# Out-projection results kept in the other half of u, PSUM banks rotated by two between stages, and another set of planner keys

## Chip, cores and metric

The kernel runs on one core of a Trainium2 chip. The metric is the device time of one execution in microseconds. Before the change it is 513.69 us (median of three runs, 512.78 to 514.52).

## What is computed

For a batch of 8, causal attention over 576 positions with 8 heads of width 64: heads 0 to 3 look at the last 32 positions (local), heads 4 to 7 at every 32nd position (strided). The eight heads side by side are x, and a gated MLP with a spatial mixing follows:

```python
scores = q @ k.T / 8, masked per head; attn = softmax(scores); x = heads of attn @ v side by side   # 576 x 512
h = relu(x @ w_in);  u, v = h[:, :512], h[:, 512:]
v_n = (v - mean(v)) / sqrt(var(v) + 1e-6)
v_s = w_spatial @ v_n + b_spatial[:, None]
out = (u * v_s) @ w_out
```

w_in, w_spatial and w_out arrive in wider types; every fp32 product is made of three fp32r matmuls (high by high, high by low, low by high), so each operand exists as a rounded half and a rest.

## The kernel before

**Stages.** Each batch b has four attention tiles (two heads each, two local and two strided) and then, on TensorE, the stages v (`project_v`, 48 matmuls of 512 columns), u (`project_u` for batches 0 and 1, `project_u_blocks` for 2 to 7), tail (`moe_tail`), s (`gate`, the spatial product times u) and o (`project_out`). From batch 2 on the order is v(b), o(b-1), u(b), the tail for every second b, s(b). Attention of the next batch or two is laid between them.

**u and o by seven products.** `project_u_blocks` and `project_out` compute a 2 by 2 block product with seven products "11", "s1", "s2", "s4", "s3", "12", "22" instead of eight. Each product is 12 matmuls of 288 columns into a pair of PSUM banks. "11", "s2", "s3" and "22" go into the pair xb, "s1" and "s4" into zb, "12" into wb. After "11" the pair xb is copied out (`keep`), and "s2" then adds on top of it in the same banks; in the same way zb is copied out after "s1" before "s4" adds to it. In u the copies after "11" are written to the first half of u, u[0] blocks 0 and 1, and those after "s1" to u[1] blocks 2 and 3. "11", "s4" and "12" of u read x directly, the others need a sum that is cast and subtracted first (`split`: a cast on ScalarE or GpSimd, L409 or L411, and a subtraction on VectorE, L419).

**Buffers.** u(b) is a pair of tiles from the ring `r_u`, which has two buffers, so u[0] of batch b has the buffer that u[0] of batch b-1 had, and u[1] that of u[1]; batch 1 has its u in two x buffers. The first access to a new tile waits for every operation on the old tile of that buffer, whichever blocks they touch (`Buf.before`). o(b-1) puts its last two results ("22", copied out of xb) into u[1] blocks 0 and 1 and stores them from there to `out` in HBM, 144 KB each.

**Banks.** The ring `r_pm` has four PSUM banks, taken in turn. In u and o, xb takes two, zb the next two; xb is held, so wb takes zb's two again. After "22" the hold is cleared, and the next stage begins with xb's banks.

**The order of everything** is made by a planner (`Program.order`) ahead of the run: each operation has a key, and each engine in turn takes the ready operation with the smallest key, where readiness is the planner's own estimate (a DMA counts as done 1600 ns and 900 ns and its transfer time after its issue). `KEYS` holds these numbers: "a" is the key of attention tiles 0 to 7 (batches 0 and 1), "la" and "lb" that of their q, k and v loads, "lv", "lu", "lo", "ls" that of the weight loads, "v", "u", "wv", "wu", "s", "t", "o" that of the conversion of the weights, "su" that of `in_weight_sums` (the sums of w_in blocks that u's products need from batch 2 on). "lead" is how long ahead of its use an attention tile from batch 2 on is due, "pre"[0] how far a `split` is put ahead of its product, "pre"[1] the same for the differences, "dp" by how much a choice of VectorE is penalised for each kind of operation. The stages of batches 0 to 7 have keys from 0 to 375; o(0) begins at 63.6, s(1) at 73.9, v(2) at 87.7 and u(2) at 108.4. Each engine and the one DMA queue (SP) then runs its list strictly in order.

Of the kernel before, what the change touches and what calls it, by code (L numbers as in the profile page):

```python
# [37 lines left out]
TAIL = S - 4 * P  # L38
NT = 4
KEYS = {  # L40
    "a": (-3398.1, -3117.71, -3291.55, -2240.6, -1996.2, 35.64, -1043.59, -1504.49,),
    "v": (691.31, 1274.34, 186.27, 627.47,),
    "u": (1079.81, 934.5, -4091.05, -677.5,),
    "s": (-2936.24, 1502.92, 3125.66, -518.81,),
    "t": (-1209.93,),
    "o": (2379.44, 1239.03,),
    "cst": (-2116.05,),
    "wv": (-860.51, -882.07, -3005.6, 768.52,),
    "wu": (1507.37, -2412.73, 850.89, 747.53,),
    "lead": (10.96,),  # L50
    "fill": (-727.48, 2496.32, -2940.02, 1257.47, 970.88, -749.94,),
    "dp": (601.61, -9631.11, 16122.32, 30415.43,),
    "dpt": (806.42,),
    "lv": (-1842.4, -1199.82, -515.75, 336.68,),
    "lu": (3197.26, 951.54, 884.39, 816.26,),
    "lo": (-770.37, -754.89, 1060.46, -3432.48,),
    "ls": (-921.47, 216.61, -1263.15, 1069.04, 606.92,),
    "pre": (1.57, 46.46,),
    "su": (-798.11,),
    "near": (3759.3,),  # L60
    "la": (-1978.67, -1285.55, -2262.03, -1136.47, -309.0, 2452.66, 231.16, 2175.93,),
    "lb": (-364.89, 1312.27, -646.09, 1254.93, 2634.11, -1849.12, -3019.6, -2748.21,),
}
WARM_END, WARM_GAP, WARM_COST, WARM_COLS, WARM_SHARE = 110000.0, 700.0, 427.0, 256, 0.8
PE_MASKED, APART = (0, 1, 2, 3), ()
# [92 lines left out]
class Program:  # L158
# [10 lines left out]
    def add(self, key, choices, fn, reads=(), writes=(), spare=None, tiled=0, port=(), kind=0):  # L169


        n = len(self.ops)
        if port:
            self.port[n] = port
        self.kind[n] = kind
        if spare is not None:
            self.spare[n] = spare
        if tiled:
            self.tiled[n] = tiled
        deps = set()  # L180
        for tok in reads:
            if tok in self.writer:
                deps.add(self.writer[tok])
            self.readers.setdefault(tok, []).append(n)
        for tok in writes:
            if tok in self.writer:
                deps.add(self.writer[tok])
            deps.update(self.readers.pop(tok, ()))
            self.writer[tok] = n
        for tok in (*reads, *writes):  # L190
            buf = tok[0]
            if isinstance(buf, Buf):
                deps.update(buf.before)
                buf.users.append(n)
        deps.discard(n)
        self.ops.append((key, choices, fn, deps))
# [143 lines left out]
def pe_cost(m, n):  # L340
    return max(m / 1.2, 4.8 + 0.4464 * n)
# [3 lines left out]
def attention_moe(ctx, tc, qT, kT, ks, vl, vs, cst, eye, w_in, w_out, wsp, wtail, out):  # L345
# [49 lines left out]
    r_pm = Ring(ps, "m", [P, 512], F32, 4)  # L395
    held, lead = set(), min(nb, 2)
# [29 lines left out]
    def evac(key, n, dst, src, reads, writes, engs=(ACT, DVE), extra=0):  # L426
        cost = {ACT: 60 + 0.833 * n + extra, DVE: 70 + 1.04 * n + extra}

        def fn(eng):
            if hasattr(eng, "activation"):  # L430
                eng.copy(dst(), src())  # L431
            else:
                eng.tensor_copy(dst(), src())

        add(key, [(e, cost[e]) for e in engs], fn, reads, writes)
# [376 lines left out]
    def x_tok(t):  # L812
        return [(xs[t], i, c0) for i in range(1 if t in WHOLE else 2) for c0 in ((0, 3) if t % NHP < 2 else (0, 1))]
# [55 lines left out]
    def split(key, n, dst, tok, val, toks):  # L869
        rnd(key, n, lambda: dst(0), val, toks, [(*tok, 0)])  # L870
        rest(key, n, lambda: dst(1), val, lambda: dst(0), toks + [(*tok, 0)], [(*tok, 1)])
# [277 lines left out]
    def project_u_blocks(b, key):  # L1149
        at, tok = sums.pop(b)  # L1150
        u = [r_u.new() for _ in range(2)]
        us[b, 0], us[b, 1] = u
        step = 1.5

        def product(key, name, src, bank, first):
            w_at, w_tok = in_sums[name]
            for r in range(2):
                op, toks = src(r, key + 0.74 * r)
                for j in range(2):

                    def fn(eng, r=r, j=j, op=op):
                        for i, (w, a) in enumerate(PROD):
                            eng.matmul(  # L1163
                                bank[j]()[:, :HS], w_at(w, r)[:, j * P : (j + 1) * P], op(a),
                                start=(first and r == 0 and i == 0), stop=(r == 1 and i == 2),
                                skip_group_check=not first,
                            )

                    add(
                        key + 0.74 * r + 0.37 * j, [(PE, 3 * pe_cost(P, HS))], fn,  # L1170
                        toks + w_tok[r], [(bank[j],)],
                    )

        def direct(k, hf):
            return lambda r, key: (
                lambda a: xs[NHP * b + 2 * k + r]()[:, a, hf * HS : hf * HS + HS], x_tok(NHP * b + 2 * k + r),
            )

        def summed(n, slot):
            def src(r, key):  # L1180
                g = gs[slot]
                op = lambda a: g()[:, 2 * r + a]
                split(key - KEYS["pre"][0], HS, op, (g, r), at(n, r), tok(n, r))
                return op, [(g, r, 0), (g, r, 1)]
            return src

        def keep(key, hf, f, bank):
            evac(key, HS, block(u[hf], f), lambda: bank()[:, :HS], [(bank,)], [(u[hf], f)])

        def join(key, hf, f, bank):  # L1190
            dst = block(u[hf], f)
            add(
                key, [(DVE, 70 + 1.04 * HS)],
                lambda eng: eng.tensor_tensor(dst(), bank()[:, :HS], dst(), op=ALU.add),  # L1194
                [(bank,)], [(u[hf], f)],
            )

        xb, zb = ([r_pm.new(held) for _ in range(2)] for _ in range(2))
        held.update(x.n % 4 for x in xb)
        product(key, "11", direct(0, 0), xb, True)  # L1200
        product(key + step, "s1", summed(0, 1), zb, True)
        for j in range(2):
            keep(key + step, 0, j, xb[j])
        product(key + 2 * step, "s2", summed(1, 0), xb, False)
        for j in range(2):
            keep(key + 2 * step, 1, 2 + j, zb[j])
        product(key + 3 * step, "s4", direct(1, 1), zb, False)
        for j in range(2):
            keep(key + 3 * step, 1, j, xb[j])
        product(key + 4 * step, "s3", summed(2, 1), xb, False)  # L1210
        for j in range(2):
            join(key + 4 * step, 1, j, zb[j])
        wb = [r_pm.new(held) for _ in range(2)]
        product(key + 5 * step, "12", direct(1, 0), wb, True)
        for j in range(2):
            join(key + 5 * step, 1, 2 + j, xb[j])
        product(key + 6 * step, "22", summed(3, 0), xb, False)
        held.clear()
        for j in range(2):
            join(key + 6 * step, 0, j, wb[j])  # L1220
            keep(key + 7 * step, 0, 2 + j, xb[j])
# [44 lines left out]
    def block(u, f):  # L1266
        return lambda: flat(u)[:, f * HS : (f + 1) * HS]
# [50 lines left out]
    def project_out(b, key):  # L1318
        u = [us.pop((b, hf)) for hf in range(2)]
# [34 lines left out]
        def keep(key, dst, bank, writes):  # L1354
            evac(key, HS, dst, lambda: bank()[:, :HS], [(bank,)], writes)
# [8 lines left out]
        def store(key, e, hf, src, reads):  # L1364
            c0 = b * S + hf * HS
            add(
                key, [(DMA, P * HS * 4 / DMA_RATE)],
                lambda eng: eng.dma_start(out[e * P : (e + 1) * P, c0 : c0 + HS], src()),
                reads, [],
            )  # L1370
# [7 lines left out]
        mine = lambda hf, f: block(u[hf], f)  # L1378
        step = 1.47
# [28 lines left out]
        xb, zb = ([r_pm.new(held) for _ in range(2)] for _ in range(2))  # L1408
# [29 lines left out]
            store(key + 5 * step, 2 + j, 1, o5[j], [(o5[j],)])  # L1438
        multiply(key + 6 * step, "22", [(0, 0), (0, 1)], xb, 0, False)
        held.clear()  # L1440
        for j in range(2):
            join(key + 6 * step, o1[j], wb[j], [(o1[j],)])
            store(key + 6 * step, j, 0, o1[j], [(o1[j],)])
        for j in range(2):
            keep(key + 7 * step, mine(1, j), xb[j], [(u[1], j)])
            store(key + 7 * step, 2 + j, 0, mine(1, j), [(u[1], j)])

    gs = []
    plan = []
# [199 lines left out]
```

## Time and profile before

| | us |
|---|---|
| median of three runs | 513.69 |
| the profiled execution | 517.83 |
| its span, first to last instruction | 515.8 |
| TensorE busy in the span | 492.4 (95%) |
| VectorE busy | 409.2 (79%) |
| ScalarE busy | 288.2 (56%) |
| GpSimd busy | 132.7 (26%) |

Times below are microseconds from the start of the span. PE is TensorE's matmul stream, PEld its weight load, DVE VectorE, ACT ScalarE, POOL GpSimd, SPq the DMA issue queue. In a timeline the figure in brackets is the idle time of the engine just before, and what ended it. Several equal instructions in a row are merged into one line, with their count.

### The profile page before, as it was taken

Reading aid. Unit: us, or ns where it says so; the run is one execution under the profiler, and the core shown is the slowest. Engines: PE = TensorE matmul, PEld = TensorE weight load, DVE = VectorE, ACT = ScalarE, POOL = GpSimd, SP = SyncE. Lnnn points to the kernel's source line nnn. Section 1 sums busy time; section 2 is a strip of 40 time slices with the busy share of each in tenths; the row PEclk is TensorE's granted clock in tenths of the full one; section 3 lists DMA queues with packets and bytes.
Section 4 is the critical chain, followed back from the end, with each engine's and each line's share of the span. In section 5 each row is a group of like instructions: output and inputs, shape, how many; then the busy total and the mean of one; then the engine's idle time right before and its main releaser. Section 6 shows DMA issues by size and latency. Waiting matters only on the chain.

```text
span 515.8 us, 16002 instructions
## 1 busy us (share of the span) xinstructions
PE 492.4 (95%) x6330; PEld 447.1 (87%) x6330; DVE 409.2 (79%) x1268; ACT 288.2 (56%) x899; POOL 132.7 (26%) x269
## 2 busy tenths in 40 slices
PE   6698999999999999999999989999899999999997
PEld 3466898898988989998998978989899998889997
DVE  4899989999999878887797947979588775658455
ACT  5797778556466738266553737527464562227314
POOL 4563343323033223121231112311122201111000
PEclk9699999999999999999999989999999999999999
DMA  8995232223421444004430244202441032001102
GB/s 292 398 376 157 74 131 81 78 89 108 155 79 48 141 132 141 17 11 139 157 122 2 71 153 128 79 0 65 143 120 32 0 97 81 1 0 61 34 0 93
DMA packets 26250, 52.71 MB, mean 102 GB/s; under 512 B 3136, under 2 KB 11584, under 8 KB 26176
## 3 DMA queue, kind: packets, MB, share of 16 engines
q1 hardware_dynamic: 26176, 51.70, 30.6%
q8 instruction: 50, 0.82, 0.7%
q14 instruction: 24, 0.20, 0.1%
HBM read 42.25 MB, written 9.44 MB: 100 GB/s over the span
## 4 chain that ended last, share of the span: by engine, by line
PE 74%; DVE 9%; DMA 7%; ACT 6%; issue 2%; SPq 1%; POOL 0%; ACTq 0%; DVEq 0%
PE m L1284 19%; PE m L1070 17%; PE m L1337 13%; PE m L1163 8%; PE m L1127 5%; PE po L616 3%; PE po L721 3%; DMA outT<-u 2%; PE s L504 2%; ACT pl L561 2%; PE m L1296 2%; PE m L1297 2%; PE s L650 2%; DVE g L419 1%; DMA vn<-w_in 1%
## 5 line engine op out<-in xcount | busy, mean ns | idle before, releaser
L1284 PE MATMUL m<-wsp_sb,vn 128*128 128x288 f32 x768 | 114.4, 297 | 1.6 <-DVE u L1194 1.5
L1284 PEld LDWEIGHTS m<-wsp_sb,vn 128*128 128x128 f32 x768 | 105.6, 188 | 4.1 <-DVE u L1194 2.4
L1070 PE MATMUL m<-w_in_sb,x 128*128 128x512 f32 (+1 forms) x408 | 99.5, 397 | 0.8 <-DVE pp L681 0.4
L1337 PE MATMUL m<-g,w_out 128*128 128x288 f32 x672 | 92.7, 296 | 1.0 <-DVE u L1360 1.0
L1337 PEld LDWEIGHTS m<-g,w_out 128*128 128x128 f32 x672 | 90.3, 188 | 2.5 <-ACT x L431 1.0
L1070 PEld LDWEIGHTS m<-w_in_sb,x 128*128 128x128 f32 (+1 forms) x408 | 74.3, 185 | 19.9 <-DVE x L419 1.0
L409 ACT CAST g<-u 128x288 fp32r<-128x288 f32 x79 | 33.9, 433 | 38.4 <-DVE u L876 20.7
L411 POOL TENSOR_SCALAR ptl<-pc 32x64 f32<-32x64 f32 (+3 forms) x92 | 36.1, 392 | 55.6 <-DVE pc L585 30.2
L1038 POOL TENSOR_TENSOR bn<-bn,cst_sb 128x1 f32<-128x1 f32 (+1 forms) x37 | 22.1, 601 | 108.4 <-DVE bn L1033 96.2
L1020 ACT ACTIVATE vv<-m 128x512 f32<-128x512 f32 (+1 forms) x37 | 21.7, 596 | 49.8 <-PE m L1070 48.7
L561 ACT ACTIVATE pl<-pl,ml 128x64 f32<-128x64 f32 (+1 forms) x140 | 47.1, 340 | 1.5 <-DVE ml L541 1.2
L419 DVE TENSOR_TENSOR g<-u,g 128x288 fp32r<-128x288 f32 x98 | 43.1, 458 | 5.7 <-ACT g L409 5.0
L431 ACT CAST x<-po 128x288 fp32r<-128x288 f32 x62 | 23.4, 402 | 36.0 <-PE po L721 28.2
L409 ACT COPY ptl<-pc 32x320 f32<-32x320 f32 (+3 forms) x100 | 35.9, 359 | 10.6 <-DVE pc L585 8.7
L1163 PE MATMUL m<-x,w_in_sb 128*128 128x288 f32 x216 | 34.6, 301 | 4.4 <-ACT u L431 4.4
L431 ACT COPY u<-m 128x288 f32<-128x288 f32 x76 | 28.1, 402 | 17.4 <-PE m L1163 7.9
L1163 PEld LDWEIGHTS m<-x,w_in_sb 128*128 128x128 f32 x216 | 29.9, 188 | 5.9 <-ACT u L431 5.1
L1025 DVE BATCH_NORM_STATS2 bn<-vv 128x6 f32<-128x512 f32 (+1 forms) x37 | 25.1, 685 | 10.5 <-ACT vv L1020 10.5
L411 POOL TENSOR_SCALAR pts<-pc 32x288 f32<-32x288 f32 x36 | 17.8, 494 | 56.5 <-PE po L721 40.5
L1045 DVE TENSOR_SCALAR vv<-vv,bn 128x512 f32<-128x512 f32 (+1 forms) x37 | 20.6, 557 | 11.8 <-POOL bn L1038 11.3
L419 DVE TENSOR_TENSOR x<-po,x 128x288 fp32r<-128x288 f32 x64 | 27.2, 447 | 2.9 <-ACT x L431 1.6
L1307 DVE SCALAR_TENSOR_TENSOR u<-u,m 128x288 f32<-128x288 f32 x48 | 21.0, 448 | 10.1 <-PE m L1297 10.1
(167 smaller groups left out, 890.6 us busy)
## 6 DMA issues: line engine op xcount, KB each, us to landing
q<-qT SPq DMA_DIRECT2D x32, 295.0 KB, 3.9
v_raw<-vs SPq DMA_DIRECT2D x15, 512.0 KB, 3.6
v_raw<-vl SPq DMA_DIRECT2D x16, 384.0 KB, 3.2
k<-kT SPq DMA_DIRECT2D x16, 304.0 KB, 4.6
kbd<-ks SPq DMA_DIRECT2D x32, 144.0 KB, 4.5
outT<-o SPq DMA_DIRECT2D x32, 144.0 KB, 3.3
outT<-u SPq DMA_DIRECT2D x28, 144.0 KB, 1.9
vn<-w_in SPq DMA_DIRECT2D x4, 512.0 KB, 6.8
```

What stands on the lines that cost most here:

```text
L409: eng.copy(dst(), src())
L411: eng.tensor_scalar(dst(), src(), 1.0, 0.0, op0=ALU.mult, op1=ALU.add)
L419: eng.tensor_tensor(dst(), src(), f32(hi()), op=ALU.subtract)
L431: eng.copy(dst(), src())
L561: eng.activation(p_sb()[:m, u, :], src, AF.Exp, bias=st()[:m, u : u + 1], scale=SCALE if masked else -1.0, **total,)
L1025: lambda eng: eng.bn_stats(bn()[:m, 0:6], v()[:m]), [(v,)], [(bn,)],
L1038: lambda eng: eng.tensor_tensor(bn()[:m, 9:10], bn()[:m, 8:9], sel[:m, 0:1], op=ALU.pow),
L1070: eng.matmul(v_ps()[:m, :], x_at(kt)[:, a, :], w_in_sb[:, w, kt, HF:], start=(n == 0 and i == 0), stop=(n == NT - 1 and i == 2),)
L1127: eng.matmul(u_ps()[:, :HS], w_in_sb[:, w, kt, f * P : (f + 1) * P], xs[NHP * b + kt]()[:, a, r], start=(n == 0 and i == 0), stop=(n == NT ...
L1163: eng.matmul(bank[j]()[:, :HS], w_at(w, r)[:, j * P : (j + 1) * P], op(a), start=(first and r == 0 and i == 0), stop=(r == 1 and i == 2), ...
L1284: eng.matmul(s_ps()[:, :HS], vn()[:, a, kt, fs], wsp_sb[:, w, kt, r], start=(kt == 0 and i == 0), stop=False,)
L1337: eng.matmul(o_ps()[:, :HS], w_out_t[0]()[:, w, r, BLOCKS[name], j * P : (j + 1) * P], at(a), start=(first and r == 0 and i == 0), stop=(r ...
```

## The change

It has three parts: in `project_out` the results of "22" go to u[0] blocks 2 and 3 and are stored from there; after the hold is cleared, in `project_u_blocks` and in `project_out`, the bank counter moves on by two, so that the next stage begins with wb's banks; and all of `KEYS` is replaced, the keys of batches 0 and 1 by those of a kernel with U as eight products.

```diff
 KEYS = {
-    "a": (-3398.1, -3117.71, -3291.55, -2240.6, -1996.2, 35.64, -1043.59, -1504.49,),
-    "v": (691.31, 1274.34, 186.27, 627.47,),
-    "u": (1079.81, 934.5, -4091.05, -677.5,),
+    "a": (-1421.69, -1241.69, -1361.69, -558.71, -62.58, 1238.23, -54.07, 892.52,),
+    "v": (-847.67, 1532.36, -699.97, -197.47,),
+    "u": (1324.65, 1473.2, 1712.36, -439.99,),
...
-    "lead": (10.96,),
+    "lead": (10.06,),
...
-    "dp": (601.61, -9631.11, 16122.32, 30415.43,),
-    "dpt": (806.42,),
-    "lv": (-1842.4, -1199.82, -515.75, 336.68,),
-    "lu": (3197.26, 951.54, 884.39, 816.26,),
+    "dp": (1410.82, -7913.25, 17481.82, 35293.8,),
+    "dpt": (1128.82,),
+    "lv": (-1086.66, -783.28, -283.36, -137.47,),
+    "lu": (1077.79, 1592.36, 778.71, 457.25,),
...
-    "pre": (1.57, 46.46,),
-    "su": (-798.11,),
-    "near": (3759.3,),
-    "la": (-1978.67, -1285.55, -2262.03, -1136.47, -309.0, 2452.66, 231.16, 2175.93,),
-    "lb": (-364.89, 1312.27, -646.09, 1254.93, 2634.11, -1849.12, -3019.6, -2748.21,),
+    "pre": (0, 63.25,),
+    "near": (4678.86,),
+    "la": (-1146.66, -1026.66, -1601.69, -759.97, -1481.69, -1206.66, 298.54, 1013.03,),
+    "lb": (-639.38, 1353.2, -257.47, 1652.36, 1178.23, 517.25, -343.36, 1784.57,),
+    "su": (72.55,),
 }
...
         product(key + 6 * step, "22", summed(3, 0), xb, False)
         held.clear()
+        r_pm.n += 2
...
         multiply(key + 6 * step, "22", [(0, 0), (0, 1)], xb, 0, False)
         held.clear()
+        r_pm.n += 2
...
         for j in range(2):
-            keep(key + 7 * step, mine(1, j), xb[j], [(u[1], j)])
-            store(key + 7 * step, 2 + j, 0, mine(1, j), [(u[1], j)])
+            keep(key + 7 * step, mine(0, 2 + j), xb[j], [(u[0], 2 + j)])
+            store(key + 7 * step, 2 + j, 0, mine(0, 2 + j), [(u[0], 2 + j)])
```

## Rows read from the trace of the kernel before

**Rows 1.** The page's first lines: the span, and TensorE's busy time.

```profile
span 515.8 us, 16002 instructions
...
PE 492.4 (95%) x6330; PEld 447.1 (87%) x6330; DVE 409.2 (79%) x1268; ACT 288.2 (56%) x899; POOL 132.7 (26%) x269
```

**Rows 2.** Busy time of each engine in six stretches of the span: the stretch, its length, then PE, PEld, DVE, ACT and POOL busy with their instructions, TensorE's granted clock as a share, the share of the 16 DMA engines, GB/s.

```profile
0.00:16.60 16.60, 8.79 (x164) 5.09 (x165) 9.22 (x24) 9.11 (x31) 5.82 (x12) 0.86 0.89 317
16.60:25.20 8.60, 8.17 (x232) 5.93 (x232) 7.27 (x17) 7.18 (x28) 6.22 (x11) 0.67 1.04 395
25.20:46.30 21.10, 19.27 (x342) 13.05 (x343) 19.76 (x55) 18.59 (x58) 11.34 (x16) 1.00 0.87 310
46.30:149.00 102.70, 101.74 (x1501) 93.94 (x1500) 96.82 (x335) 68.89 (x229) 34.33 (x66) 1.00 0.32 103
149.00:512.40 363.40, 354.48 (x4099) 329.06 (x4097) 276.09 (x842) 183.98 (x554) 75.03 (x166) 1.00 0.24 73
512.40:515.80 3.40, 0.00 (x0) 0.00 (x0) 0.00 (x0) 0.41 (x2) 0.00 (x0) 1.00 0.34 115
```

**Rows 3.** What TensorE's matmul stream waited for over the whole span: waiting line and releaser, us in total, times, longest us.

```profile
PE m L504 <- DMA vn<-w_in: 6.0, 1, 6.0
PE m L1163 <- ACT u L431: 4.4, 3, 2.2
PE m L1284 <- DVE u L1194: 1.5, 4, 0.4
...
PE m L1337 <- DVE u L1360: 1.0, 1, 1.0
```

**Rows 4.** All engines in order of time from the end of o(3) into u(4); of these lines those of PE, ACT's copies out of PSUM and SPq's stores. PE's lines at 294.43, 295.21 and 297.60 are the first half of "s1", "11" and, after the other half of "s1", "s2"; 301.57 is the beginning of "s4".

```profile
294.43 0.94 PE L1163 MATMUL m<-g,v_raw 128*128 128x288 f32 x6
...
295.21 1.76 PE L1163 MATMUL m<-x,w_in_sb 128*128 128x288 f32 x12
...
296.48 0.98 SPq L1368 DMA_DIRECT2D outT<-u  x2
...
296.93 0.67 ACT L431 COPY u<-m 128x288 f32<-128x288 f32 x2
...
297.60 1.77 PE L1163 MATMUL m<-g,su_sb 128*128 128x288 f32 x12
...
301.12 0.70 ACT L431 COPY u<-m 128x288 f32<-128x288 f32 x2 [2.85 <-DMA outT<-u]
...
301.57 0.66 PE L1163 MATMUL m<-x,w_in_sb 128*128 128x288 f32 x3 [2.20 <-ACT u L431]
```

**Rows 5.** TensorE alone in order of time: a place in o(0); the beginning of "s4" in u(3); the attention product behind the wait of rows 4; the beginning of "s4" in u(5), and the same attention product there; the beginning of u(6) and of its "s4", and the same of u(7).

```profile
127.88 3.40 PE L1337 MATMUL m<-g,w_out 128*128 128x288 f32 x24 [0.96 <-DVE u L1360]
...
241.47 0.66 PE L1163 MATMUL m<-x,w_in_sb 128*128 128x288 f32 x3 [0.80 <-ACT u L431]
...
302.18 2.19 PE L616 MATMUL po<-ptl,v_raw 128*64 128x96 f32 x24
...
365.75 0.66 PE L1163 MATMUL m<-x,w_in_sb 128*128 128x288 f32 x3 [1.37 <-ACT u L431]
366.36 1.21 PE L616 MATMUL po<-ptl,v_raw 128*64 128x96 f32 x24
...
417.73 0.56 PE L1163 MATMUL m<-g,v_raw 128*128 128x288 f32 x3
...
422.50 0.55 PE L1163 MATMUL m<-x,w_in_sb 128*128 128x288 f32 x3
...
475.05 0.56 PE L1163 MATMUL m<-g,v_raw 128*128 128x288 f32 x3
...
479.81 1.76 PE L1163 MATMUL m<-x,w_in_sb 128*128 128x288 f32 x12
```

**Rows 6.** ScalarE's copies after "s1" in u(6) and u(7), and the last stores of o(6) ahead of u(7), from the same view.

```profile
421.55 0.70 ACT L431 COPY u<-m 128x288 f32<-128x288 f32 x2
...
476.52 0.92 SPq L1368 DMA_DIRECT2D outT<-u  x2
...
479.05 1.36 ACT L431 COPY u<-m 128x288 f32<-128x288 f32 x4 [0.19 <-DMA outT<-u]
```

**Rows 7.** The end of u(3) and the beginning of s(3), all engines in order of time: the last matmuls of "12" and those of "22", the copies out of xb (ACT), the additions from wb (DVE L1194), the first matmuls of s(3).

```profile
248.65 1.47 PE L1163 MATMUL m<-x,w_in_sb 128*128 128x288 f32 x9
...
249.95 1.76 PE L1163 MATMUL m<-g,w_in_sb 128*128 128x288 f32 x12
...
251.51 0.69 ACT L431 COPY u<-m 128x288 f32<-128x288 f32 x2
251.56 0.81 DVE L1194 TENSOR_TENSOR u<-m,u 128x288 f32<-128x288 f32 x2
252.07 2.13 PE L1284 MATMUL m<-wsp_sb,vn 128*128 128x288 f32 x14 [0.35 <-DVE u L1194]
```

**Rows 8.** VectorE in order of time near the end of o(0): a sum of w_in blocks (L876 on vv) and the two additions that o(0) waits for.

```profile
125.54 0.76 DVE L876 TENSOR_TENSOR vv<-w_in_sb 128x256 f32<-128x256 f32 x2
...
127.28 0.82 DVE L1360 TENSOR_TENSOR u<-m,u 128x288 f32<-128x288 f32 x2
```

**Rows 9.** DMA issues by line: count, size of one, median us from issue to landing.

```profile
vn<-w_in SPq DMA_DIRECT2D x4, 512.0 KB, 6.8
```

**Rows 10.** VectorE's groups by line, the subtractions behind the casts of o's operands: count, busy us, mean ns of one, idle time before them and what ended it.

```profile
L419 DVE TENSOR_TENSOR g<-u,g 128x288 fp32r<-128x288 f32 x98 | 43.1, 458 | 5.7 <-ACT g L409 5.0 <-POOL g L411 0.4
```

More of the change, by code (lines that the diff above doesn't have):

```diff
@@ L40 @@
 KEYS = {
-    "a": (-3398.1, -3117.71, -3291.55, -2240.6, -1996.2, 35.64, -1043.59, -1504.49,),
-    "v": (691.31, 1274.34, 186.27, 627.47,),
-    "u": (1079.81, 934.5, -4091.05, -677.5,),
[L44 to L49, printed above, removed]
-    "lead": (10.96,),
-    "fill": (-727.48, 2496.32, -2940.02, 1257.47, 970.88, -749.94,),
-    "dp": (601.61, -9631.11, 16122.32, 30415.43,),
-    "dpt": (806.42,),
-    "lv": (-1842.4, -1199.82, -515.75, 336.68,),
-    "lu": (3197.26, 951.54, 884.39, 816.26,),
-    "lo": (-770.37, -754.89, 1060.46, -3432.48,),
-    "ls": (-921.47, 216.61, -1263.15, 1069.04, 606.92,),
-    "pre": (1.57, 46.46,),
-    "su": (-798.11,),
-    "near": (3759.3,),
-    "la": (-1978.67, -1285.55, -2262.03, -1136.47, -309.0, 2452.66, 231.16, 2175.93,),
-    "lb": (-364.89, 1312.27, -646.09, 1254.93, 2634.11, -1849.12, -3019.6, -2748.21,),
+    "a": (-1421.69, -1241.69, -1361.69, -558.71, -62.58, 1238.23, -54.07, 892.52,),
+    "v": (-847.67, 1532.36, -699.97, -197.47,),
+    "u": (1324.65, 1473.2, 1712.36, -439.99,),
+    "s": (1012.52, 598.55, 1017.79, -966.66,),
+    "t": (-499.99,),
+    "o": (2286.8, 1318.36,),
+    "cst": (-1301.69,),
+    "wv": (881.01, 658.55, 952.52, 1146.71,),
+    "wu": (-591.56, -379.99, 1013.62, 150.66,),
+    "lead": (10.06,),
+    "fill": (543.23, 1772.36, 1844.57, 1298.23, 718.55, 1316.97,),
+    "dp": (1410.82, -7913.25, 17481.82, 35293.8,),
+    "dpt": (1128.82,),
+    "lv": (-1086.66, -783.28, -283.36, -137.47,),
+    "lu": (1077.79, 1592.36, 778.71, 457.25,),
+    "lo": (2266.42, 802.57, 2267.81, 800.73,),
+    "ls": (-699.38, 821.01, -907.67, -122.58, 778.55,),
+    "pre": (0, 63.25,),
[3 more added lines that the diff above has]
+    "su": (72.55,),
 }
```

## Prediction

> **What bounds the kernel now.** I read the busy shares first, then the table of six stretches, then TensorE's waits, then the order of time around each wait that comes more than once. TensorE is busy 95% of the span [rows 1]; the reader is to see where the other 5% lies. In the table [rows 2] length less PE busy is 7.81 + 0.43 + 1.83 = 10.1 us before 46.3 us, 1.0 from there to 149, 8.9 from 149 to 512.4, and 3.4 at the end, where only the last copy and store run: 23.4, the span minus 492.4. So from 46.3 us on the kernel is bound by TensorE, and an edit there is worth at most the waits that it removes. Before 46.3 us the DMA engines are busy 0.87 to 1.04 of the time and the granted clock falls to 0.67 in one stretch: there loads and conversions decide, in the order of the keys. The list of waits [rows 3] has three that the change touches: 4.4 us in u for copies of ScalarE (three times), 1.5 us at the beginning of s (four times), 1.0 us in o(0).
>
> **Part 1, the banks.** At the end of u the first tile of s takes the bank xb[0], which "22" has just filled. In u(3) [rows 7] "22" starts at 249.95, the copy of xb[0] at 251.51 takes 0.35 (0.69 for two), and s begins at 252.07 after 0.35 idle. Four of these make the 1.5 us. After the change s begins in wb's bank. Its product "12" ended near 250.1, 1.5 us before, and what is left is the addition on VectorE. So the wait goes if that addition is done before "22" ends. Here it is not: it starts at 251.56 because VectorE serves the attention's operations first, and its first half ends at 251.97, behind the copy's 251.86. If VectorE's order stays, the new wait is 0.1 longer: 4 x 0.1 = +0.4. If attention moves by its new lead (0.9 later, out of the way of an addition 0.41 long), all of it goes: -1.5. I take -1.5, since the addition has 1.4 us between "12" and the copy and needs 0.41, and keep +0.4 as the other end. At the beginning of u after o the rotation removes nothing: the planner already runs half of "s1" there first, in wb's banks, and TensorE is back at once (294.43) [rows 4]. What is late next at s is the second tile's bank, which is ready 0.4 us after the first, while the first tile's products take 1.5.
>
> **Part 2, the half of u.** The 4.4 us are a store's. At 296.48 two stores of o(3)'s last results are issued from u[1] blocks 0 and 1 [rows 4]. ScalarE's copies to u[0] at 296.93 run at once; those to u[1] blocks 2 and 3 wait 2.85 us until the stores land, start at 301.12, and "s4" starts 0.45 later, 2.20 us late. So a new tile waits for the stores of the old one even where the blocks differ, and the other half does not. With the last results in u[0], the wait moves to the copies after "11", which "s2" needs. Those come one product earlier in the list. What that costs depends on what TensorE finds meanwhile. From the end of o, "11" and "s1" take 3.2 us (294.43 to 297.60) [rows 4]. If "s2" stands next in the list, it starts at the same 301.57 with one product of 1.6 us less done. If the planner, which counts a store as landed 2.5 us and more after its issue, finds "s2" not ready and puts "s4" (x direct, its copies in u[1] now free) ahead of it, three products are done when the stores land, exactly as before. I take this one: 0, because the list goes by readiness first; the other end is worked out with the rival below, and the gain is bounded by -5.4: the three waits (0.80, 2.20, 1.37) [rows 4, 5] and 1.0 of slower clock behind the longest, where the attention product takes 2.19 instead of 1.21 [rows 5]. A gain would need the stores to land earlier, and their queue is not touched except by keys. In o itself u[0] blocks 2 and 3 are read last by the casts for "12", one product before they are overwritten; that is 1.6 us for a cast and subtraction of 0.4 each: nothing. At the end of the kernel the last copy and store are the same: 3.4 us stay.
>
> The Trainium skill ("DMA: Bandwidth & Descriptors", section "Anatomy of one DMA", on the gpsimd path) says that a DMA's semaphore fires only after the last byte is confirmed written, about 2 us as a constant cost and longest towards HBM. It speaks against this part: what is stored last should lie where it is overwritten last. The trace agrees in kind, though these stores go by another queue: from the second issue's end, 297.46, to the waiting copy at 301.12 it is 3.66 us [rows 4], more than the page's constant.
>
> **Part 3, the keys.** "su" goes from -798 to 72.55, behind o(0) (63.6). In o(0) TensorE waits 0.96 us [rows 5] for additions that VectorE starts at 127.28, with weight sums such as the pair at 125.54 (0.76 us) ahead of them [rows 8]. With the sums behind, I count -1.0; they are needed by u(2) only, and the cover is VectorE's idle time from 149 on (276 of 363 busy) [rows 2]. If it fails, the 1.0 stays. "pre"[0] goes from 1.57 to 0, so casts no longer outrank the copies and additions of the same product. TensorE hardly waits for them now (none in [rows 3]; VectorE waits 5.0 us in 98 subtractions for ScalarE's casts [rows 10]). Taken as 0. Bounds: nothing below; above, if 0.1 us shows in each of six products with operands of eight o stages, +4.8. The casts have left VectorE, so a higher "dp" has nothing to move: 0. "lead" makes attention due 0.9 later: taken as 0 but for part 1. The order of batches 0 and 1 is the large unknown. The first loads by key stay nearly the same (tile 2's q, the constants, tile 0's, the first quarter of w_in's v half, tile 1's k); behind them w_in's second and third quarters come ahead of the wider spread of before, and tiles 7 and 5 fall behind nearly all else. One load of 512 KB [rows 9] at 395 GB/s [rows 2] is 1.33 us in a stretch where the DMA engines are full; three loads in another order give 4.0 us either way. I take 0 and keep -4 and +4.
>
> **The sum.** Banks -1.5, half of u 0, sums -1.0, the rest 0: -2.5 us. Against the profiled execution of 517.83 (515.8 of span and 2.03 around it) that is 515.3; the median is 4.1 below that execution, so I put the difference on the median: 513.69 - 2.5 = 511.2. Of this kernel about 0.3%, 1.5 us, can be told from no change, so "same" reaches from 512.15 to 515.2.
>
> **Rivals.**
> - *"s2" waits for the stores in full.* The place is the copy after "11" in u(3) to u(7); it decides if the planner's list has "s2" next after "s1". Then u(3), u(4) and u(5) each lose a product more, 3 x 1.6 = 4.8. In u(7), which begins at 475.05 [rows 5], the stores of 476.52 land at 479.05 [rows 6], "s2" would be ready 0.45 later and TensorE would be there at 475.05 + 3.2 = 478.2: 1.3. In u(6), from 417.73 on, the copies at 421.55 show no wait, so at most 422.0 - 420.9 = 1.1; I take 0.7. Waits of 3.8, 2.4 and 3.0 us would each cost the 1.0 of clock that the 2.2 cost, two more than now: 2.0. Sum 8.8, and with the -2.5: 520.0; without clock 518.0. Against it: readiness is what the list goes by, and "s4" is ready.
> - *The new keys are worse at the start or the casts come late.* +4.0 of loads or +4.8 of casts, with the -2.5: about 515.5, up to 516.5.
> - *The new keys are better at the start.* -4.0: 507.2. For it: 10.1 us of idle TensorE, of which 6.0 is one wait for DMA [rows 3].
> - *The change doesn't do what it says.* The additions from wb still stand behind attention (+0.4), the weight sums only move the wait: 513.7 to 514.1.
>
> **How the numbers follow.** Forecast 0.40 (510 to 513), the store rival 0.20 (517 to 520.5), the worse keys 0.15 (514.5 to 517.5), the better keys 0.15 (505.5 to 509), no effect 0.10. Faster: 0.15 and most of the forecast, 0.33: 0.48. Same: 0.10 + 0.07 + 0.02 = 0.19. Slower: 0.20 + 0.13 = 0.33. Cases of both signs hold the chance; the forecast's own range is 510 to 513. The range 506 to 519 leaves out the lower edge of the better keys and the upper half of the store rival, some 0.15.
>
> **What would show it.** In the profile after: at the beginning of u(3) to u(5) "11" comes first, then "s1", then "s4" before "s2", and ScalarE's copies to u[0] carry the wait for DMA; if "s2" stands third, the store rival holds. At the beginning of s no wait for a copy, and the addition from wb done before "22" ends. In o(0) no weight sum ahead of the additions. Up to the first s matmul of batch 0 the time shows what the keys did to the start. Wrong would be: waits of TensorE in the out-projection for VectorE's subtractions, or stores that land at another time than now.

## The result and the profile after

| | before | after |
|---|---|---|
| median, us (runs) | 513.69 (5) | 517.17 (5), from 516.48 to 518.58 |
| ratio to before, 95% interval | | 1.0058 [1.0030, 1.0086] |
| the profiled execution, us | 517.83 | 516.48 |
| its span, us | 515.8 | 514.7 |

The change makes the kernel 0.6% slower, 3.0 us by the ratio. The two profiles say the opposite, since the profiled execution of before lay 4.1 above its median and that of after 0.7 below its own. So sizes below come from ratios over many runs, and the profiles are used for places. Three single executions of 937, 1186 and 2121 us, one each of `places_only`, `keys_half` and `keys_su`, are left out of the ratios as slow.

The page's first lines and three stretches of after, in the columns of [rows 1] and [rows 2]:

```profile
span 514.7 us, 15962 instructions
...
PE 492.5 (96%) x6326; PEld 447.4 (87%) x6326; DVE 403.7 (78%) x1264; ACT 293.9 (57%) x913; POOL 125.1 (24%) x259
```

```profile
25.20:46.30 21.10, 21.10 (x396) 16.48 (x390) 19.02 (x55) 17.95 (x55) 8.80 (x14) 1.00 0.88 306
46.30:149.00 102.70, 100.06 (x1477) 91.95 (x1476) 94.83 (x331) 70.25 (x233) 31.30 (x60) 0.98 0.31 97
149.00:512.40 363.40, 355.20 (x4102) 328.47 (x4101) 273.61 (x844) 188.59 (x568) 72.19 (x160) 1.00 0.25 75
```

The keys fill TensorE in 25 to 46 us (21.10 busy instead of 19.27), and lose it again before 149: idle 2.6 us where it was 1.0. The waits, as in [rows 3]:

```profile
PE m L504 <- DMA q<-qT: 7.2, 1, 7.2
PE m L1338 <- DVE u L1361: 2.5, 1, 2.5
PE m L1285 <- ACT u L431: 2.0, 3, 0.7
PE m L1163 <- ACT u L431: 1.6, 3, 0.6
PE s L504 <- DMA k<-kT: 0.9, 1, 0.9
...
PE m L1070 <- DVE u L1194: 0.7, 2, 0.4
```

(The bank lines shift the code by one: L1338 is [rows 5]' L1337.) The wait for u's copies fell from 4.4 to 1.6 us. Three others grew: o(0) from 1.0 to 2.5, the beginning of s, or of the tail where that comes first, from 1.5 to 2.7 (the lines L1285 and L1070), and a new one of 0.9 in front of attention scores. (The first line, the wait for the first loads, was 6.0 before; in a second profile of each kernel it is 6.8 before and 6.6 after.) The wait of 0.9 stands in u(4), at the place of [rows 4]. TensorE there in after, and then ScalarE's copies and SPq's stores:

```profile
294.31 1.76 PE L1163 MATMUL m<-x,w_in_sb 128*128 128x288 f32 x12
295.91 1.74 PE L1163 MATMUL m<-g,v_raw 128*128 128x288 f32 x12
298.60 1.10 PE L504 MATMUL s<-k,q 64*32 64x64 f32 x72 [0.95 <-DMA k<-kT]
299.63 0.67 PE L1163 MATMUL m<-x,w_in_sb 128*128 128x288 f32 x3
300.94 0.66 PE L1163 MATMUL m<-g,su_sb 128*128 128x288 f32 x3 [0.64 <-ACT u L431]
301.55 0.72 PE L616 MATMUL po<-ptl,v_raw 128*64 128x96 f32 x12
302.19 0.66 PE L1163 MATMUL m<-g,su_sb 128*128 128x288 f32 x3
302.78 0.72 PE L616 MATMUL po<-ptl,v_raw 128*64 128x96 f32 x12
```

```profile
296.31 0.87 SPq L1369 DMA_DIRECT2D outT<-u  x2
297.48 0.67 ACT L431 COPY u<-m 128x288 f32<-128x288 f32 x2
300.49 0.70 ACT L431 COPY u<-m 128x288 f32<-128x288 f32 x2 [2.34 <-DMA outT<-u]
```

The copies after "11" wait for the stores, as expected. But ahead of "s2" (su_sb) stand attention scores and only three of the twelve matmuls of "s4" (the second x line), where I had put a whole product. The scores come before their keys have been loaded and wait 0.95 us; the attention product is cut in two.

### The profile page after: what moved, and what is told of

It reads as the page before. It is cut to its first block, busy times and chain, and to the rows that moved or that the text cites. A ratio compares the mean times of both kernels' runs of the same rounds, so it can differ in the third digit from the quotient of the medians.

```text
span 514.7 us, 15962 instructions
## 1 busy us (share of the span) xinstructions
PE 492.5 (96%) x6326; PEld 447.4 (87%) x6326; DVE 403.7 (78%) x1264; ACT 293.9 (57%) x913; POOL 125.1 (24%) x259
## 4 chain that ended last, share of the span: by engine, by line
PE 76%; DVE 9%; DMA 6%; ACT 5%; issue 2%; POOL 1%; SPq 1%; ACTq 0%; POOLq 0%; DVEq 0%
PE m L1285 18%; PE m L1070 17%; PE m L1338 13%; PE m L1163 9%; PE m L1127 5%; PE po L721 4%; PE po L616 3%; DMA outT<-u 2%; DMA kbd<-ks 2%; PE s L650 2%; DMA q<-qT 2%; PE s L504 2%; PE m L1297 2%; PE m L1298 1%; ACT pl L561 1%
## 5 line engine op out<-in xcount | busy, mean ns | idle before, releaser
L1285 PE MATMUL m<-wsp_sb,vn 128*128 128x288 f32 x768 | 113.9, 297 | 2.2 <-ACT u L431 2.0
L1285 PEld LDWEIGHTS m<-wsp_sb,vn 128*128 128x128 f32 x768 | 105.4, 188 | 4.2 <-ACT u L431 2.7
L1070 PE MATMUL m<-w_in_sb,x 128*128 128x512 f32 (+1 forms) x408 | 98.3, 396 | 0.0
L1338 PE MATMUL m<-g,w_out 128*128 128x288 f32 x672 | 93.4, 298 | 2.6 <-DVE u L1361 2.5
L1338 PEld LDWEIGHTS m<-g,w_out 128*128 128x128 f32 x672 | 91.1, 190 | 4.3 <-ACT xt L409 2.6
L1070 PEld LDWEIGHTS m<-w_in_sb,x 128*128 128x128 f32 (+1 forms) x408 | 74.4, 185 | 17.8
L409 ACT CAST g<-u 128x288 fp32r<-128x288 f32 x83 | 35.9, 434 | 37.8 <-DVE u L876 21.1
L411 POOL TENSOR_SCALAR ptl<-pc 32x64 f32<-32x64 f32 (+3 forms) x95 | 37.6, 395 | 59.0 <-DVE pc L585 33.5
L419 DVE TENSOR_TENSOR g<-u,g 128x288 fp32r<-128x288 f32 x98 | 42.9, 454 | 6.7 <-ACT g L409 3.3
L431 ACT CAST x<-po 128x288 fp32r<-128x288 f32 x64 | 24.3, 398 | 35.8 <-PE po L721 24.3
L409 ACT COPY ptl<-pc 32x320 f32<-32x320 f32 (+3 forms) x97 | 34.6, 356 | 10.8 <-DVE pc L585 9.1
L431 ACT COPY u<-m 128x288 f32<-128x288 f32 x76 | 28.5, 399 | 14.3 <-DMA outT<-u 5.1
L411 POOL TENSOR_SCALAR pts<-pc 32x288 f32<-32x288 f32 x32 | 14.9, 467 | 55.2 <-PE po L721 26.7
```

Source lines behind the costliest of these rows:

```text
L411: eng.tensor_scalar(dst(), src(), 1.0, 0.0, op0=ALU.mult, op1=ALU.add)
L419: eng.tensor_tensor(dst(), src(), f32(hi()), op=ALU.subtract)
L1070: eng.matmul(v_ps()[:m, :], x_at(kt)[:, a, :], w_in_sb[:, w, kt, HF:], start=(n == 0 and i == 0), stop=(n == NT - 1 and i == 2),)
L1285: eng.matmul(s_ps()[:, :HS], vn()[:, a, kt, fs], wsp_sb[:, w, kt, r], start=(kt == 0 and i == 0), stop=False,)
L1338: eng.matmul(o_ps()[:, :HS], w_out_t[0]()[:, w, r, BLOCKS[name], j * P : (j + 1) * P], at(a), start=(first and r == 0 and i == 0), stop=(r ...
```

## Experiments

Each ratio is to runs of the kernel before on the same chip, taken together with them (33, 35 and three times 17 of them, medians 514.0 to 515.3), with its 95% interval. Times in us are the ratio times that median.

### Which part costs

Both kernels once more, then each part of the diff alone or with one other: `KEYS` (keys), `r_pm.n += 2` twice (banks), the last hunk (half). `places_only` is half and banks with the keys of before; `half_only`, for instance, is:

```diff
-            keep(key + 7 * step, mine(1, j), xb[j], [(u[1], j)])
-            store(key + 7 * step, 2 + j, 0, mine(1, j), [(u[1], j)])
+            keep(key + 7 * step, mine(0, 2 + j), xb[j], [(u[0], 2 + j)])
+            store(key + 7 * step, 2 + j, 0, mine(0, 2 + j), [(u[0], 2 + j)])
```

> The kernel before once more, unchanged, for a second profile beside the first, whose execution (517.83 us) lies 4.1 above the median. Theory S (the landing of o's last stores differs from execution to execution): ratio 1.000, span about 511 to 513, and the waits of ScalarE's copies for stores (6.5 us in the first profile) fall to under 3 us. Theory H (the start differs from execution to execution): the same ratio, the store waits stay near 6 us and u(0) begins 2 us or more earlier than 46.3.

> The changed kernel once more, for a second profile. Both theories: ratio 1.003 to 1.009. The wait in o(0) stays 2.5 us with a slow clock behind it (it belongs to the order); the first store wait of u(3) to u(5) varies between 0 and 2 us each.

> Only the keys are changed. Theory K (the keys cost the time: a start that is 3 us better, given back by the end of o(0) and more): ratio 1.005 to 1.008, with o(0)'s wait of 2 us or more. Theory P (the places cost it: the half of u and the banks): ratio 0.995 to 1.001.

> The half of u and the banks are changed, with the keys of before. Theory P: ratio 1.004 to 1.008, a store wait of 0.5 us or more in each of u(3) to u(7) and a wait for xb or wb at the beginning of each s. Theory K: ratio 0.998 to 1.002.

> Only the half of u is changed; keys and banks as before. Theory A (the half costs the places' 1.2 us: the list puts attention's scores and part of "s4" between "s1" and "s2" of u(3) to u(7), the scores wait for their k load or a chain of VectorE, and the attention product comes later): ratio 1.002 to 1.004, u(6) 14.5 us or more instead of 13.7. Theory B (the banks cost it): ratio 0.999 to 1.001.

> Only the bank counter is changed. Theory A: ratio 0.999 to 1.001; at the beginning of each s a wait of 0.35 to 0.7 us remains, now for the addition from wb. Theory B (s's first tile waits longer, for an addition behind attention on VectorE): ratio 1.002 to 1.004.

> The new keys with the half of u, banks as before. Theory A with an extra cost where the keys and the half meet (u(4), 17.8 to 19.0 us against 16.4 to 17.0 with one of them): ratio 1.005 to 1.008, u(4) over 17.5 us. Theory B: ratio 1.001 to 1.003, as with the keys alone.

> The new keys with the other bank order, half as before. Theory A: ratio 1.000 to 1.003, as with the keys alone. Theory B: ratio 1.004 to 1.007.

| kernel | ratio | interval |
|---|---|---|
| before again | 1.0000 | 0.9983 to 1.0017 |
| after again | 1.0065 | 1.0043 to 1.0086 |
| half | 1.0057 | 1.0036 to 1.0078 |
| banks | 1.0001 | 0.9978 to 1.0024 |
| keys | 1.0018 | 0.9994 to 1.0041 |
| half, banks | 1.0024 | 1.0006 to 1.0042 |
| keys, half | 1.0053 | 1.0031 to 1.0075 |
| keys, banks | 1.0016 | 0.9989 to 1.0043 |

The half of u by itself costs as much as the whole change, +2.9 us. Banks give nothing, keys +0.9, which can't be told from zero. Why `places_only` is cheaper than `half_only` stays open; their intervals overlap by a little.

Not every expectation held. The half cost more than theory A said (1.002 to 1.004), `keys_only` and `places_only` lie between their two theories, and the copies' waits for stores in before again are 4.1 us, not under 3. With banks alone the wait at the beginning of s is for the copies from xb and not for the addition from wb; what that means is said under "The beginning of s".

Where the 2.9 lie can be seen by adding up the batches, each from its u to the next, in one profiled execution of each kernel: from the first matmul of u(2) to the first of o(7) it is 324.1 us in the mean of seven kernels with the last results in u[1] (322.8 to 327.3) and 326.1 in that of five with them in u[0] (325.3 to 327.5). Of these 2.0, batch 4 has 1.1, batches 5, 6 and 7 have 0.3, 0.6 and 0.4, batches 2 and 3 together -0.4. The store waits themselves vary from execution to execution (4.4 us in before, 3.0 in before again, 1.1 with banks alone), and are not larger with the half. In u(6) of `half_only` no copy waits for a store, and still time is lost at its end (TensorE's "22", ScalarE, the next stage):

```profile
427.78 1.75 PE L1163 MATMUL m<-g,w_in_sb 128*128 128x288 f32 x12
...
429.55 0.30 ACT L409 CAST xt<-x 128x128 fp32r<-128x128 f32 x1 [0.70 <-DVE x L419]
429.75 0.69 ACT L431 COPY u<-m 128x288 f32<-128x288 f32 x2
...
430.20 1.65 PE L1070 MATMUL m<-w_in_sb,xt 128*128 128x512 f32 x6 [0.67 <-ACT u L431]
```

With another order of products, attention's last product stands six matmuls ahead of "22" instead of three, and a cast of its result now comes ahead of the copies of xb in ScalarE's list. It waits 0.70 us for VectorE, and the next stage starts 0.67 late; in the kernel before that wait is not there at u(6). Behind u(3), u(4) and u(5) the same wait is 0.67 or 0.68 us, where it was 0.35 or 0.36. In all, the waits at the beginning of the stage after u are 3.0 us in `half_only` and 1.5 in the kernel before, so by these profiles about half of the 2.9 lies there.

### The store, the order, or the place

`own_tiles` puts the last two results of each o into two tiles of the v stage's ring (vv), which is idle then, and stores from there. `own2` does so from o(2) on only:

```diff
+        o7 = [r_vv.new() for _ in range(2)] if b >= 2 else None
...
+            last, at = mine(1, j), (u[1], j)
+            if o7:
+                last, at = (lambda v=o7[j]: v()[:, :HS]), (o7[j],)
-            keep(key + 7 * step, mine(1, j), xb[j], [(u[1], j)])
-            store(key + 7 * step, 2 + j, 0, mine(1, j), [(u[1], j)])
+            keep(key + 7 * step, last, xb[j], [at])
+            store(key + 7 * step, 2 + j, 0, last, [at])
```

> The kernel before (its keys, its banks), with the last two results of the out-projection copied to two tiles of the ring of the v stage (vv), idle during o and u, and stored from there. No copy of u then waits for a store, and TensorE's list in u(2) to u(7) is, operation for operation, that of the kernel before. Theory W (the store waits are a price paid in the kernel before, about equal with either half of u): the waits of TensorE for ScalarE's copies in u, 3.0 to 4.4 us in its two executions, go, with about 1 us of slow clock in u(4): ratio 0.990 to 0.994, 509 to 511 us. Rival V (the waits only hide something else, such as the attention products or VectorE's sums that would be late anyway): the idle time turns up behind attention or at the beginning of s, ratio 0.998 to 1.000.

> The kernel before with the last two results of o(2) to o(7) in two tiles of the vv ring (o(0) and o(1) stay as they were, so that the list of batches 0 and 1 is untouched). The lists of TensorE and VectorE are those of the kernel before, operation for operation; only ScalarE, GpSimd and the DMA queue have a few entries in another order. Theory W (in own_tiles u(3) to u(5) became 4.6 us shorter, and the loss lay in batches 0 and 1 alone): u(3) to u(5) take 15.2 to 15.5 us each, no wait for a copy behind a store, ratio 0.990 to 0.993 (509 to 510.5). Rival V (what the stores no longer take turns up elsewhere): 0.997 to 1.002.

`own_tiles`: 1.0088 [1.0064, 1.0112], against both theories. Its u(3) to u(5) took 15.5, 15.2 and 15.2 us (before again: 16.8, 16.9, 16.5), so the store's wait did go. The loss is elsewhere: o(0)'s use of vv gave the planner another order in batches 0 and 1, where s(1) waits for VectorE:

```profile
147.30 3.01 PE L1284 MATMUL m<-wsp_sb,vn 128*128 128x288 f32 x11 [5.53 <-DVE x L1310]
```

`own2`, whose TensorE and VectorE lists are those of before, operation for operation: 0.9922 [0.9897, 0.9947], 510.87 us, 4.0 below before: theory W. (Its u(4) and u(5) took 15.2 us each as expected, its u(3) 16.2, with a wait of 0.93 for a load of attention's values.) At the place of [rows 4] (PE, ACT's copies, SPq's stores):

```profile
295.12 1.76 PE L1163 MATMUL m<-x,w_in_sb 128*128 128x288 f32 x12
295.44 1.01 SPq L1368 DMA_DIRECT2D outT<-vv  x2
296.72 0.96 PE L1163 MATMUL m<-g,v_raw 128*128 128x288 f32 x6
296.83 1.29 ACT L431 COPY u<-m 128x288 f32<-128x288 f32 x4
297.52 1.78 PE L1163 MATMUL m<-g,su_sb 128*128 128x288 f32 x12
298.97 0.76 ACT L431 COPY u<-m 128x288 f32<-128x288 f32 x2
299.13 0.56 PE L1163 MATMUL m<-x,w_in_sb 128*128 128x288 f32 x3
299.62 1.21 PE L616 MATMUL po<-ptl,v_raw 128*64 128x96 f32 x24
```

"s4" follows "s2" without a wait, and the attention product behind it takes 1.21 us instead of 2.19 [rows 5].

`half_free` keeps the copies in u[0] but lets the stores read another tile; `half_third` keeps copies and stores, and makes the planner count these stores as done when issued:

```diff
# half_free
             keep(key + 7 * step, mine(0, 2 + j), xb[j], [(u[0], 2 + j)])
+            last, at = (o1[j], (o1[j],)) if b >= 2 else (mine(0, 2 + j), (u[0], 2 + j))
+            store(key + 7 * step, 2 + j, 0, last, [at])
# half_third, in order()
                 done, free[e] = streamed + DMA_TAIL, now + DMA_ISSUE
+                if n in self.soon:
+                    done = now
```

> The half of u alone, but from batch 2 on the last two stores of an o read the tiles of o1 instead of u (so two of its eight blocks of out hold other rows). The copies stay in u[0]; only the stores leave u free, and then the planner's lists for TensorE and VectorE are those of the kernel before, operation for operation. Theory X (the half costs only through the store: the planner counts u[0] as not ready and brings scores and s4 forward): like own2, ratio 0.990 to 0.994. Rival Y (the copies in u[0] cost by themselves, by the casts of 12 or the order of ScalarE): above own2 by 0.003 or more.

> The half of u alone, with the planner told that these two stores of o(2) to o(7) land at once. Its lists for TensorE, VectorE and the DMA queue are then those of the kernel before, operation for operation, so s2 stands behind s1 again, and on the chip its copies wait for the stores. The rival of the prediction priced that at +8.8 us with slower clock, +6.8 without: ratio 1.013 to 1.017. If instead the stores land before the copies after 11 matter (theory Z, the list alone made the half slow), ratio 0.998 to 1.003.

`half_free`: 0.9925 [0.9898, 0.9952], as `own2`: without the store the place costs nothing, theory X. `half_third`: 1.0197 [1.0171, 1.0223], +10.1 us. In its u(4), with TensorE's list of before ("11", half of "s1", "s2"), ScalarE's copies and TensorE, and then the granted clock (first share) behind:

```profile
298.83 1.14 SPq L1371 DMA_DIRECT2D outT<-u  x2
...
302.65 1.31 ACT L434 COPY u<-m 128x288 f32<-128x288 f32 x4 [2.69 <-DMA outT<-u]
303.10 3.25 PE L1166 MATMUL m<-g,su_sb 128*128 128x288 f32 x12 [2.38 <-ACT u L434]
```

```profile
303.00:306.40 3.40, 3.30 (x14) 3.30 (x15) 1.11 (x4) 2.29 (x11) 0.43 (x1) 0.52 0.00 0
```

The wait of 2.38 us is followed by a granted clock of 0.52, nearly all of it at the lower level of 1.2 GHz, and "s2" takes 3.25 us instead of 1.78. Together 3.9, and the batches with u(3), u(4) and u(5) are 4.1 us longer each than in `half_free`. This is the prediction's store rival, measured. The planner's new order avoids it, and comes out 2.9 us above the kernel before. No run has that new order without the stores' waits, so how the 2.9 divide between the order and the waits that are left is not shown.

### The beginning of s

`half_early` is the half, `own_early` is `own_tiles` with banks, both with u's last additions and copies made urgent:

```diff
-            join(key + 6 * step, 0, j, wb[j])
-            keep(key + 7 * step, 0, 2 + j, xb[j])
+            join(key - 60, 0, j, wb[j])
+            keep(key - 60, 0, 2 + j, xb[j])
```

> The half of u alone (ratio 1.0057 by itself), with the same four operations of u made urgent. Theory Q: what the half costs in u(6) and u(7) and at the beginning of s (waits of 0.66 to 0.9 us for the copies queued behind attention) goes for the most part: ratio 1.001 to 1.003, waits at the beginning of s below 0.3. Theory L (the list itself costs: scores and part of s4 come forward where their operands are not ready, and every wait stays somewhere): ratio 1.004 to 1.007.

> own_tiles with the change's banks and, in u from batch 2 on, the last two additions from wb and the last two copies from xb made urgent (key - 60), so that they go ahead of attention's copies and subtractions on ScalarE and VectorE. Theory Q (at the beginning of s TensorE waits because those two operations queue behind attention's work, whichever bank it takes): the four waits of 0.36 to 0.68 us at the beginning of s fall below 0.2 each and the ratio is 0.002 to 0.004 below that of own_tiles. Rival R (the attention work pushed back is itself due): the waits move to attention's products, ratio equal to own_tiles within 0.002.

`half_early`: 1.0019 [0.9997, 1.0041], +1.0 us where `half_only` has +2.9, theory Q by its numbers: no wait at the beginning of any s after u(3) to u(6). But what it pushed back is due elsewhere: in s(4) it waits 1.38 us for a load of attention's strided keys, 0.26 and 0.53 for VectorE. In `own_early`, 1.0235 [1.0204, 1.0266], the waits at the beginning of s are gone too, and attention's come instead, up to 1.84 us inside "22":

```profile
318.95 1.74 PE L721 MATMUL po<-pts,v_raw 64*64 64x36 f32 x64 [1.84 <-DMA v_raw<-vs]
```

So rival R held, and more than it said: 7.6 us above `own_tiles`, and u(4) with s(4) alone is 9.1 us longer in its profile (an execution 3.8 above its median). And banks alone? The wait of [rows 7] did not shrink:

```profile
249.75 1.25 PE L1163 MATMUL m<-g,w_in_sb 128*128 128x288 f32 x8
251.62 1.61 PE L1285 MATMUL m<-wsp_sb,vn 128*128 128x288 f32 x10 [0.63 <-ACT u L431]
```

It is 0.63 us instead of 0.35, and something else ends it. In [rows 7] that is the addition from wb (DVE L1194), here the copy from xb (ACT L431). So TensorE began s in wb's bank before the change, and begins it in xb's bank with the rotation. The ring does give the first tile of s xb's bank before and wb's after, as was said ahead. But the planner's list begins s(3) with three matmuls of its third tile, whose bank is two further on, because it estimates that bank to be free first; in both traces the first three matmuls wait for one engine and the next twelve for the other. The rotation exchanges the two waits; it removes neither.

### The keys

`su_only` is before with `su` alone, `keys_su` the new keys with the old `su`, `keys_t5` the new keys with attention tile 5 and its loads as early as before:

```diff
# su_only; keys_su is the reverse in the new KEYS
-    "su": (-798.11,),
+    "su": (72.55,),
# keys_t5, in the new KEYS: a[5], a[7]; also la[6], la[7], lb[4], lb[5], lb[7]
-    "a": (-1421.69, -1241.69, -1361.69, -558.71, -62.58, 1238.23, -54.07, 892.52,),
+    "a": (-1421.69, -1241.69, -1361.69, -558.71, -62.58, 35.64, -54.07, -40.0,),
```

> The kernel before with su alone at 72.55, behind o(0). The lists of all engines but VectorE are unchanged, and VectorE has eight places in another order. The prediction gave this -1.0 us: the wait of 0.96 in o(0) goes, ratio 0.998. Rival: the weight sums were not what the additions waited for, the wait stays at 0.9 to 1.0 us, ratio 1.000.

> The new keys alone (1.0018) with su put back to -798.11. TensorE's list is that of the new keys, operation for operation; VectorE has nine places in another order. Theory C (the weight sums, put behind o(0), now meet VectorE's full stretch and made o(0)'s wait grow from 0.96 to 2.5 us): the wait falls to 1.0 or below, ratio 0.997 to 0.999. Theory D (VectorE is full there because attention tile 5 comes late, whatever the sums do): the wait stays at 2.3 to 2.8 us, ratio 1.000 to 1.003.

> The new keys alone (ratio 1.0018 by themselves), with the keys of attention tiles 5 and 7 and of their loads and of tile 6's brought forward to those of the kernel before in kind (a[5] 1238 to 36, a[7] 893 to -40). Theory N (the new keys put tile 5's chain so late that VectorE idles at 80 to 112 and is full at 112 to 131, which makes o(0) wait 2.5 us and the clock there fall to 0.86): VectorE is busier in 80 to 112, o(0) waits under 1.2 us, granted clock 1.0 there, and the 4 us won at the start are kept in part: ratio 0.995 to 0.999. Rival M (the start is bound by loads and VectorE's sum of work up to o(1), whatever the order): o(1) begins when it did, ratio 1.000 to 1.003.

`su_only`: 0.9992 [0.9974, 1.0011], the wait in o(0) is 0.96 us as before. VectorE runs the same sums ahead of the same additions as in [rows 8]:

```profile
126.61 0.75 DVE L876 TENSOR_TENSOR vv<-w_in_sb 128x256 f32<-128x256 f32 x2
...
128.35 0.82 DVE L1360 TENSOR_TENSOR u<-m,u 128x288 f32<-128x288 f32 x2
```

`keys_su`: 0.9996 [0.9972, 1.0020], the wait stays at 2.52 (theory D by the wait; the ratio is just below its range). VectorE is the engine that it waits for. In 80 to 112 us it has less to do under the new keys (28.06 us busy; the first line is `keys_only`, the second before again), and from 112 to 131 it is busy for 18.90 of 19.00:

```profile
80.00:112.00 32.00, 32.00 (x425) 27.94 (x425) 28.06 (x87) 22.41 (x70) 12.94 (x26) 1.00 0.31 99
112.00:131.00 19.00, 16.29 (x229) 15.32 (x228) 18.90 (x56) 11.17 (x30) 2.00 (x4) 0.91 0.29 93
```

```profile
80.00:112.00 32.00, 32.00 (x387) 29.12 (x379) 30.82 (x94) 21.17 (x65) 12.00 (x22) 1.00 0.31 100
112.00:131.00 19.00, 18.04 (x301) 16.23 (x301) 18.01 (x56) 11.03 (x29) 5.15 (x8) 1.00 0.32 100
```

`keys_t5` was to show that tile 5 is at fault: 1.0215 [1.0186, 1.0243], against both theories. The wait in o(0) fell to 0.44, but 2.65 us follow at attention's product, and u(2) begins at 180.0 instead of 174.4 (`keys_only`). So that VectorE is full when o(0) needs it is shown; that tile 5's place is the cause, and that putting it back would help, is not.

### The parts together

`after_own` is the changed kernel with `own2`'s edit in place of the half.

> The changed kernel (its keys, its banks) with the half of u put back and the last two results of o(2) to o(7) in two tiles of the vv ring, as in own2. Theory A (the parts add: the half's place was the only loss of the change, and the keys and banks are worth about nothing): keys with banks had 1.0016, own2 0.9922, so 0.994, 510.5 to 512. Rival B (with the store out of the way the keys of the change are worth more, or cost what the stores' waits hid): 0.989 or below, or 0.998 and above. No wait for a copy behind a store in u either way.

`after_own`: 0.9933 [0.9908, 0.9958], 511.28 us: theory A. With the store off u, the change's keys and banks are worth nothing measurable, and `own2` without them is as fast.

## Why the prediction was wrong

- **The sign was wrong, by part 2.** The step was "three products are done when the stores land, exactly as before. I take this one: 0". The mechanism was half right: the copies to u[0] do wait, and the planner, counting the store as not landed, puts other work ahead of "s2". But that work is not one product of "s4". It is scores whose own operands can be late (a wait of 0.95 us in u(4) of the changed kernel, 0.30 in `half_only`), only three matmuls of "s4" in u(3) to u(5) and nine in u(6) and u(7), and another order of attention's work at the end of u, which makes the next stage wait 0.67 us. Measured +2.9. The cost of the new order was taken as nothing because the count of products was the same; what the replaced work waits for was not looked at.
- **The sum.** Of the -2.5, the half of u was 0 and is +2.9, the banks were -1.5 and are about 0, the sums of w_in were -1.0 and are -0.4; the last two can't be told from zero.
- **The store rival** was priced at +8.8 for a list with "s2" third. Such a list costs +10.1 (`half_third`). Its terms were right in kind: the waits, which I put at 3.8, 2.4 and 3.0 and are 2.28 to 2.38, and the slow clock behind each, which I put at 1.0 and is 1.4 to 1.5. The list of the changed kernel is not this one, so that its 517.17 lies in the range I gave this rival (517 to 520.5) is chance.
- **The gain bound of -5.4** for waits that disappear: taking the store off u gives -4.0 (`own2`). The bound sums the waits of one execution, 4.4 us; in before again they are 3.0.
- **Banks, -1.5: the premise was wrong.** I had s wait for the copy from xb. [rows 7] already names the addition from wb (DVE L1194) as what ends the wait: s begins at 252.07, behind the first half of that addition (251.97). The rotation put the copy in its place. The waits at the beginning of s and of the tail are 2.4 us in the profile of banks alone instead of 1.5, the time is the same (1.0001). Both the additions and the copies still queue behind attention's operations, and the lead key moved nothing out of their way.
- **Sums, -1.0: wrong.** The key does not move the sums that stand ahead of the additions [rows 8], and VectorE is busy for 18.01 of 19.00 us around them in before again. Under the other new keys the wait even grew, to 2.5, with either `su`.
- **Start keys, 0 with -4 and +4: right as a size, by luck.** The keys do win: u(0) begins at 42.9 us in after again, at 46.8 in before again. All of it is given back by o(1), which begins at 161.9 and 161.7; nothing in the prediction says so. "pre" at 0: TensorE shows no wait for a cast of o, as forecast. The rival of worse keys adds up to 515.2 and 516.0, not 515.5 and 516.5.
- **The anchor** was right: the difference belonged on the median, not on the profiled execution.

The Trainium skill's sentence that the prediction weighed ("DMA: Bandwidth & Descriptors", section "Anatomy of one DMA", on the gpsimd path) is that the semaphore comes only after the last byte is confirmed, and that this is most of a fixed cost of about 2 us. It spoke against this part, and the runs bear it out in kind; the times here are longer, the transfer included. From the end of the second store's issue to the waiting copy it was 2.68 us in `half_third` (299.97 to 302.65) and 3.31 in after (297.18 to 300.49). And `half_free` shows that the place costs nothing but this wait for the store and what the planner does about it.

## What to carry to other kernels

When a buffer is stored from and then reused, the question is not which half holds the stored data but whether the next user has to touch that buffer at all: two idle tiles elsewhere gave 0.8%, the other half of the same buffer lost 0.6%. Where a planner orders by estimated readiness, a delayed operand costs what the work pulled ahead of it waits for, so read that work's own operands before calling the swap free. And compare instruction lists before timing an edit: the three runs that left the lists of TensorE and VectorE alone (`own2`, `half_free`, `half_third`) came out within 1.5 us of what a theory said; `own_tiles` and `keys_t5`, which disturbed batches 0 and 1, came out 4.5 and 11 us above before for reasons of their own. And read what ended a wait: the name in [rows 7] would have corrected the premise on the banks.

## What was not expected of the hardware

The store's landing differs from execution to execution: the three waits of u(3) to u(5) are 0.80, 2.20 and 1.37 us in one execution of the kernel before and 0.56, 1.47 and 1.00 in another.

A wait of TensorE of 2.2 to 2.7 us was followed by a lower granted clock in most cases, not in all. It was 0.50 to 0.54 behind the three waits of "s2" in `half_third` (2.28 to 2.38 us; 12 matmuls took 3.16 to 3.25 us instead of 1.78). It was 0.50 over the attention product behind the 2.20 of [rows 4], which took 2.19 instead of 1.21, and the scores after it took 1.34 instead of 0.97. So in these four cases in u the wait cost about 1.6 times itself. Behind 1.47 us in before again it stayed 1.00.

In o(0) the same length of wait did not act in the same way. Over the 24 matmuls behind 2.52 us the clock was 0.71 in after and 1.00 in `keys_su`, and the matmuls took 4.83 us both times, because at the full clock TensorE waited once more for VectorE:

```profile
125.98 2.17 PE L1337 MATMUL m<-g,w_out 128*128 128x288 f32 x12 [2.52 <-DVE u L1360]
128.99 1.82 PE L1337 MATMUL m<-g,w_out 128*128 128x288 f32 x12 [0.84 <-DVE o L1360]
```

The lower clock cost nothing there. Why it fell in the one and not in the other is not shown.
